# Attention before a mixture of experts: five instruction queues in one fixed table per pair of heads, clusters chosen for two heads at once

## The chip, the cores and the metric

The program runs on one core of one Trainium2 chip. The metric is the device time of one execution in microseconds (us), lower is better. Five engines work side by side, each through its own queue in order: PE (TensorE, the matmuls), DVE (VectorE), ACT (ScalarE), POOL (GpSimd) and SP (SyncE, which here only issues DMAs). In the profile PEld are PE's weight loads and SPq and POOLq are the DMA-issuing parts of SP and POOL.

## The reference

Three stages follow each other. The first is attention in which a query sees only the keys of its own cluster; its output feeds a dense layer (512 to 2048 and back) and a mixture of 8 experts.

```python
B, H, S, D, n_clusters = 2, 8, 768, 64, 16
q_assign = argmax(q_n @ c_n.T, axis=-1)         # nearest of 16 centroids, per head
k_assign = argmax(k_n @ c_n.T, axis=-1)
mask = q_assign[:, :, :, None] == k_assign[:, :, None, :]
scores = where(mask, q @ k.T / sqrt(D), -1e9)
attn = exp(scores - max(scores)); attn /= attn.sum(-1) + 1e-9
x = attn @ v                                     # then x -> [B*S, H*D] = [1536, 512]
x = silu(x @ moe_w_in) @ moe_w_out
out = sum over 8 experts of P[:, e] * (relu(x @ w1[e]) @ w2[e])   # P: Sinkhorn-normalised gate
```

## The kernel before

There are 16 heads (2 batches of 8). A head has 768 queries and 768 keys, and its scores are worked on in six tiles of 128 queries by 768 keys; the whole attention stage is 96 such tiles. Two heads make a pair, and the output of a pair fills 128 rows of the transposed activations `xh`, `xl` (a rounded number and its remainder, as everywhere in this kernel where float32 accuracy is reached with two fp32r operands).

The steps of a head, with the names that the profile shows and their lines:

- `load` (L137, L139) brings keys and queries to `raw` (128 x 768: 64 rows of keys, 64 of queries) and the values to `vr`. `cast` scales the queries on POOL (L155), rounds by a DMA from POOL's queue (L156) to slot 2 of `qk`, and copies the other slots by three DMAs on SP (L158, L159). `split` takes the remainder on POOL (L169) and places it with two DMAs on SP (L170, L171).
- `assign` (L219): similarity `sim` of each of six groups of 128 positions with the head's centroids: the 128 x 128 block of `raw` is the stationary operand, 32 columns of `chl` (the centroids of keys and of queries) move. `choose` (L232 to L237) takes the maximum over 16, marks it, picks one mark and writes `oh`, a one-hot row per position.
- `mask_transp` (L243) turns `oh` with six PE transposes into `oht`, of which 48 rows are used, and `mask_rows` copies 16 rows of it into slot 3 and, scaled by 2**60 and shifted by -2**60, 16 rows into slot 2 of `qk` (ACT, L248 and L252; DVE L250 for head 0). These 16 extra contraction rows put the mask into the scores.
- `scores` (L269, L270): four matmuls of 384 columns for a tile, two for each half of the keys: one with 128 contraction rows, one with 80, of which the last 16 are the mask. The tile `s` lies in one of two PSUM buffers. `rowmax` (DVE L275) and `expo` (ACT L284) follow, and the exponentials free the PSUM buffer. When both tiles of a chunk are through, `normalise` works out `rec` (DVE L289, L290) and scales `p` on POOL (L293).
- `transp` (PE L303): three units of four 128 x 128 transposes per chunk, through three PSUM buffers `t`; `evac` copies them to `pt` (two units on ACT, one on DVE).
- `av` (L334): for each third of the queries 12 matmuls (24 instructions in the profile) with 64 stationary columns, the two heads of a pair alternating; then `xh` on ACT (L346) and `xl` on DVE (L347).

What sets the order: the main loop at the end of the stage walks over the tiles and calls the steps at fixed distances before the head that needs them (`AHEAD`), and the scheduler of the framework then places the instructions on each engine by its own estimate of when they are ready, in this stage and the next. `SEQ` runs the tiles of heads 0 and 1 one after the other and from then on alternates between the two heads of a pair by thirds. The first weight block of the dense layer is fetched and split in this stage as well (`wload`, `narrow`, `wsplit`): two of its four pieces in the first 35 us.

After the stage the pools are closed and the dense layer begins (L456, `l`), then the experts (L706).

## Time and profile before

| | |
|---|---|
| runs of the program | 1538.35, 1540.16, 1540.43 us; median 1540.16 us |
| the profiled execution | 1541.73 us |
| its span, from the first to the last instruction | 1539.9 us |
| mean granted TensorE clock | 0.998 |
| attention, up to the first matmul of the dense layer | 288.27 us |
| dense layer and experts | 1251.6 us |
| busy share of the span | PE 97%, PEld 86%, DVE 70%, ACT 59%, POOL 32% |

The profile gives the instructions of one execution with start and duration, and for each idle stretch of an engine what ended it. A PE duration includes the passage through the array, so durations of matmuls that follow each other overlap; the distance from start to start is what one of them costs in a row of many. The granted clock is the share that the throttle grants; whether the array runs at its lower level (1.2 GHz) or its higher (2.4 GHz) shows in that distance.

### The profile page before, as it was taken

The numbers are of one execution on the slowest core, as the hardware profiler recorded it, in microseconds if no ns is written. First come the engines' busy times: TensorE is split into PE (matmuls) and PEld (weight loads), VectorE is DVE, ScalarE is ACT, GpSimd is POOL, SyncE is SP. The second block draws the span as 40 slices with busy tenths as digits, with TensorE's granted clock in tenths as the row PEclk, the third lists the DMA queues.
The fourth block names the chain that finished last, engine by engine and source line by source line (L and its number), as shares of the span: only waits on it lengthen the run. The fifth ranks groups of instructions, "written<-read, shape, count | busy, mean of one in ns | idle before, by whom it ended". The sixth has DMA issues, their size and how long they took to land.

```text
span 1539.9 us, 24994 instructions
## 1 busy us (share of the span) xinstructions
PE 1495.0 (97%) x9768; PEld 1328.9 (86%) x9768; DVE 1080.1 (70%) x1680; ACT 910.0 (59%) x1732; POOL 485.8 (32%) x429
## 2 busy tenths in 40 slices
PE   5999999999999999999899999999999999999997
PEld 4777777777888878999899999999999999999997
DVE  5765666689778268877586685775776866866857
ACT  3766767432342337575665765865766756757654
POOL 5765554465665400125411211201201202112111
PEclk9999999999999999999999999999999999999999
DMA  6444442122110102668877958759759559569575
GB/s 205 138 131 122 123 109 98 29 69 96 55 55 1 55 1 74 154 114 224 151 132 141 147 94 157 128 96 174 114 95 188 96 104 193 86 120 166 87 138 103
DMA packets 131334, 175.66 MB, mean 114 GB/s; under 512 B 5456, under 2 KB 100944, under 8 KB 131216
## 3 DMA queue, kind: packets, MB, share of 16 engines
q0 software_dynamic: 82976, 86.91, 36.9%
q1 hardware_dynamic: 48096, 87.13, 17.9%
q8 instruction: 77, 1.26, 0.3%
q14 instruction: 41, 0.34, 0.1%
q10 hardware_dynamic: 144, 0.03, 0.0%
HBM read 64.54 MB, written 88.87 MB: 100 GB/s over the span
## 4 chain that ended last, share of the span: by engine, by line
PE 82%; DVE 8%; POOL 4%; DMA 2%; issue 2%; ACT 1%; POOLq 0%; DVEq 0%; SPq 0%; ACTq 0%
PE b L706 29%; PE a L706 29%; PE l L456 13%; PE av L334 3%; PE t L303 3%; PE s L269 2%; PE s L270 1%; DVE m L275 1%; DMA out_dram<-acc 1%; PE sim L219 1%; POOL p L293 1%; POOL raw L169 1%; ACT p L284 1%; PE gl L649 0%; DVE acc L794 0%
## 5 line engine op out<-in xcount | busy, mean ns | idle before, releaser
L819 POOL DMA_DIRECT2D out_dram<-acc x101 | 146.6, 1724 | 755.8 <-ACT acc L813 503.8
L706 PE MATMUL b<-wfh,ah 128*128 128x256 f32 x1344 | 381.9, 284 | 2.2 <-ACT acc L813 1.8
L706 PE MATMUL b<-wfl,ah 128*128 128x256 f32 x1344 | 381.3, 284 | 0.2 <-DVE wfl L529 0.2
L706 PE MATMUL b<-wfh,al 128*128 128x256 f32 x1344 | 381.1, 284 | 0.0
L706 PE MATMUL a<-xfh,wfh 128*128 128x512 f32 (+1 forms) x896 | 303.6, 339 | 4.2 <-ACT acc L813 1.8
L706 PE MATMUL a<-xfl,wfh 128*128 128x512 f32 (+1 forms) x896 | 303.1, 338 | 0.0
L706 PE MATMUL a<-xfh,wfl 128*128 128x512 f32 (+1 forms) x896 | 301.8, 337 | 0.9 <-DVE wfl L529 0.9
L706 PEld LDWEIGHTS b<-wfh,ah 128*128 128x128 f32 x1344 | 258.3, 192 | 3.6 <-ACT acc L813 2.3
L706 PEld LDWEIGHTS b<-wfl,ah 128*128 128x128 f32 x1344 | 258.3, 192 | 0.9 <-DVE wfl L529 0.4
L706 PEld LDWEIGHTS b<-wfh,al 128*128 128x128 f32 x1344 | 258.3, 192 | 0.0
L813 ACT ACTIVATE acc<-b,Pg 128x256 f32<-128x256 f32 x484 | 188.3, 494 | 30.7 <-issue 18.8
L756 ACT CAST ah<-h 128x768 fp32r<-128x768 f32 x192 | 159.0, 862 | 66.4 <-DVE h L838 26.3
L706 PEld LDWEIGHTS a<-xfh,wfh 128*128 128x128 f32 x896 | 170.3, 190 | 24.3 <-ACT acc L813 2.5
L529 DVE TENSOR_TENSOR al<-h,ah 128x768 fp32r<-128x768 f32 x192 | 177.2, 957 | 19.4 <-ACT ah L756 18.8
L706 PEld LDWEIGHTS a<-xfh,wfl 128*128 128x128 f32 x896 | 169.9, 190 | 19.9 <-DVE wfl L529 1.4
L706 PEld LDWEIGHTS a<-xfl,wfh 128*128 128x128 f32 x896 | 170.4, 190 | 16.7
L529 DVE TENSOR_TENSOR wfl<-w0r,wfh 128x512 fp32r<-128x512 f32 x96 | 64.8, 689 | 82.4 <-ACT wfh L604 80.3
L526 DVE TENSOR_TENSOR h<-a,h 128x512 f32<-128x512 f32 x144 | 94.2, 685 | 26.7 <-PE a L706 25.6
L275 DVE TENSOR_REDUCE m<-s 128x1 f32<-128x768 f32 x96 | 91.4, 953 | 29.6 <-PE s L270 28.7
L284 ACT ACTIVATE p<-s,m 128x768 f32<-128x768 f32 x96 | 86.9, 906 | 40.1 <-DVE rec L290 16.5
L293 POOL TENSOR_SCALAR p<-p,rec 128x768 f32<-128x768 f32 x96 | 86.8, 915 | 71.4 <-DVE rec L290 43.7
L743 ACT COPY h<-a 128x512 f32<-128x512 f32 x144 | 80.7, 591 | 45.6 <-PE a L706 45.5
(189 smaller groups left out, 2693.4 us busy)
## 6 DMA issues: line engine op xcount, KB each, us to landing
out_dram<-acc POOLq DMA_DIRECT2D x101, 768.0 KB, 9.9
w0r<-in_w_dram SPq DMA_DIRECT2D x16, 1024.0 KB, 8.1
w1r<-in_w_dram SPq DMA_DIRECT2D x16, 1024.0 KB, 6.8
qk<-qk SPq DMA_DIRECT2D x45, 192.0 KB, 3.3
raw<-in_w_out_dram SPq DMA_DIRECT2D x8, 1024.0 KB, 4.9
raw<-in_kq_dram SPq DMA_DIRECT2D x16, 384.0 KB, 3.8
raw<-in_w_in_dram SPq DMA_DIRECT2D x6, 1024.0 KB, 5.2
out_dram<-acc SPq DMA_DIRECT2D x8, 768.0 KB, 4.0
```

The source lines that it names most:

```text
L275: nc.vector.tensor_reduce(out=m, in_=tiles[i]["s"][:, :, :CH], axis=AX.XY, op=ALU.max, negate=True)
L284: nc.scalar.activation(p, t.pop("s")[:, :, :CH], AF.Exp, bias=t.pop("m"), accum_out=chunks[c]["sum"][:, j : j + 1])
L293: nc.gpsimd.tensor_scalar(out=p, in0=p, scalar1=ck["rec"][:, j : j + 1], scalar2=1.0, op0=ALU.mult, op1=ALU.mult)
L303: nc.tensor.transpose(ps[:, b * P : (b + 1) * P], p[:, kt * P : (kt + 1) * P], ident)
L456: nc.tensor.matmul(ps, lhsT=s(k), rhs=m(k), start=n == 0, stop=n == 11)
L526: e.tensor_tensor(out=out, in0=in0, in1=in1, op=op)
L529: e.tensor_tensor(out=lo, in0=x, in1=r(hi), op=ALU.subtract)
L706: nc.tensor.matmul(ps[bank][:, cols], lhsT=lf(i, k), rhs=rt(j, k), start=first and bank not in opened, stop=k == 1 and q == 2, skip_group_ ...
L743: act.copy(bank(t, u), ps[u])
L756: act.copy(hi, x)
L813: act.mul(t[:, 2 * u + m], z[:, m], g)
L819: gps.dma_start(out=out_block(i, j), in_=t, accum_op=ALU.add)
```

## The change

Only the attention stage is touched. The order of the instructions of dense layer and experts is the same, row for row, on every engine.

1. The stage is written by hand for all five queues, SP's included, and no longer placed by the scheduler. A text table `ORDER` names 135 steps; it is the same for each pair of heads. An entry `T,-6` in pair k is step number 18k - 6 of its kind, so that entries with negative numbers finish the pair before, and `sim,1`, `castm,4` and the like prepare the next pairs. `where_is` alternates the heads of a pair from the first pair on.
2. The similarity of both heads is taken together (`simil`): now the centroids are stationary, 32 columns, and `raw` moves, 384 columns at a time; the four results go to four strips of 32 partitions of one PSUM bank. A copy to SBUF (`sims`) and three transposes (`simt`) bring it to positions by rows, and `cha` to `che` choose for both heads in operations of twice the width.
3. `oh` holds both heads in 128 columns: six transposes (`oht`) per pair in place of twelve. One ACT operation (`mr`) scales all 128 rows into `mk` in SBUF, and four DMAs of 16 rows (`md`, on SP) place them in the `qk` slots. The mask row is now -2**60 times "not in this cluster" instead of a scaled and shifted one-hot row.
4. `scores` cuts the 768 keys into 512 and 256 columns instead of twice 384.
5. Of the 18 transposed units of a pair 11 are copied by ACT and 7 by DVE (before 12 and 6). Buffers: `raw` 4 (before 3), `vr` 6 (5), `pt` 4 (6).
6. The prologue issues 12 matmuls on a constant tile (`warm`), and 12 more at four places before the first scores, and 4 after each of tiles 1 and 3 (`FILL`). `make_identity`, the cast of it and the constants stand in another order, and the two early weight pieces leave the prologue: all four pieces are fetched and split, one per pair, in pairs 1 to 6.

```diff
-    SEQ = [(g, t) for g in range(2) for t in range(NCH)] + [(g + o, t) for g in range(2, NH, 2) for t in range(NCH) for o in range(2)]
+    def where_is(c):
+        k, o = divmod(c, 2)
+        pair, third = divmod(k, NTHIRD)
+        return 2 * pair + o, third
...
-        for i in range(NT):
-            nc.tensor.matmul(
-                hd["sim"][:, i].rearrange("p a c -> p (a c)"),
-                lhsT=hd["raw"][:, i * P : (i + 1) * P],
-                rhs=chl[:, hd["h"]].rearrange("p a c -> p (a c)"),
...
+    def simil(q, where=False):
+        ps = half_bank(q, "sim", where and q > 1)
+        for j in range(2):
+            for o in range(2):
+                row = 32 * (2 * j + o)
+                cl = chl[:, (2 * q + o) % H].rearrange("p a c -> p (a c)")
+                nc.tensor.matmul(ps[row : row + 32, :CH], lhsT=cl, rhs=raw[2 * q + o][:, j * CH : (j + 1) * CH], start=True, stop=True, skip_group_check=True)
+        sim[q] = ps
+
+    def sims(q):
+        t = ap.tile([P, CH], F32, name=f"sims{q}", tag="sims", bufs=1)
+        nc.scalar.copy(t, sim[q][:, :CH])
+        sim[q] = t
+
+    def simt(q, where=False):
+        ps = half_bank(q, "simt", where)
+        for b in range(CH // P):
+            nc.tensor.transpose(ps[:, b * P : (b + 1) * P], sim[q][:, b * P : (b + 1) * P], ident)
...
+    def oht(q, where=False):
+        po = half_bank(q, "oht", where).bitcast(BF16)
         for i in range(NT):
+            nc.tensor.transpose(po[:, i * P : (i + 1) * P], onehot[q % 2][:, 2 * (i % 3) + i // 3, :], identb)
+        rows[q] = po
+
+    def mr(q):
+        mk = ap.tile([P, S], F32R, name=f"mk{q}", tag="mk", bufs=1)
+        nc.scalar.activation(mk, rows.pop(q)[:, :S], AF.Copy, scale=msc)
+        rows[q] = mk
+
+    def md(q):
+        mk = rows.pop(q)
+        for o in range(2):
+            for a, slot in enumerate((3, 2)):
+                row = 64 * o + 32 * a
+                nc.sync.dma_start(out=r(qk[2 * q + o][D : D + C, slot, :]), in_=r(mk[row : row + C]))
...
-        for c in range(2):
-            nc.tensor.matmul(ps[:, c, :CH], lhsT=t[:, 1, qt * P : (qt + 1) * P], rhs=t[:, 0, c * CH : (c + 1) * CH], start=True, stop=False)
-            nc.tensor.matmul(ps[:, c, :CH], lhsT=t[: D + C, 3, qt * P : (qt + 1) * P], rhs=t[: D + C, 2, c * CH : (c + 1) * CH], start=False, stop=True)
+        for ks in (slice(0, 512), slice(512, S)):
+            nc.tensor.matmul(ps[:, ks], lhsT=t[:, 1, qt * P : (qt + 1) * P], rhs=t[:, 0, ks], start=True, stop=False)
+            nc.tensor.matmul(ps[:, ks], lhsT=t[: D + C, 3, qt * P : (qt + 1) * P], rhs=t[: D + C, 2, ks], start=False, stop=True)
...
+    ORDER = """
+        S,0 xh,-2 xl,-2 nrm,-2 T,-6 mx,0 T,-5 nrm,-1 S,1 evA,-5 evD,-6 ex,0 T,-4 mx,1 castm,4 sim,1,1 T,-3 evA,-4 wp1,-3 ex,1 T,-2 evD,-3 T,-1 sims,1
...
+    with tc.manual_schedule(engines={ENG.PE, ENG.DVE, ENG.Activation, ENG.Pool, ENG.SP}):
...
+        def warm(n):
+            for _ in range(n):
+                nc.tensor.matmul(wps, lhsT=wm[:, :P], rhs=wm, start=True, stop=True)
+
+        FILL = {1: 4, 3: 4}
+        PTB = 4
+        warm(12)
+        make_identity(nc, ident)
...
+        for pair in range(-4, NPAIR + 4):
+            for item in ORDER:
+                kind, at, *place = item.split(",")
+                f, stride, low, high = KINDS[kind]
+                i = int(at) + stride * pair
+                if low <= i < high:
+                    f(i, *(bool(int(w)) for w in place))
```

How the rows move. First PE at the very start of the program; in these rows `s` are scores, `pc` the transposed centroids, `sim` similarities, `oht` the transposed one-hot rows, `wm` and `wps` the constant tile and its target. Before, from the first instruction:

```order
L269 MATMUL s_194<-qk_109 128x384
L269 MATMUL s_235<-qk_109 128x384
L200 MATMUL pc<-ident,cn_134 128x128
L219 MATMUL sim_161<-chl,raw_93 128x32 x6
L243 LDWEIGHTS oh_143
L243 MATMUL oht_175<-identb,oh_143 48x128
```

Now, from the last of the first 12 constant matmuls on:

```order
L398 LDWEIGHTS wm
L398 MATMUL wps<-wm 128x512
L446 MATMUL pc<-ident,cn_175 128x128
L398 LDWEIGHTS wm
L398 MATMUL wps<-wm 128x512
L189 MATMUL sim_183<-raw_90,chl 32x384
L189 MATMUL sim_183<-raw_92,chl 32x384
L189 MATMUL sim_183<-raw_90,chl 32x384
L189 MATMUL sim_183<-raw_92,chl 32x384
```

Before, the first halves of two score tiles stood ahead of everything and the similarities of head 0 came alone, those of heads 1 and 2 after its `oht`. Now no scores stand there, and four matmuls serve heads 0 and 1 together.

Second, PE in the middle of the stage, where the similarities of a later head or pair are taken; `t` are the transposed exponentials. Before:

```order
L303 MATMUL t_1378<-ident,p_1288 128x128 x4
L269 MATMUL s_1393<-qk_843 128x384
L270 MATMUL s_1393<-qk_843 128x384
L269 MATMUL s_1393<-qk_843 128x384
L270 MATMUL s_1393<-qk_843 128x384
L219 MATMUL sim_1408<-chl,raw_1274 128x32 x6
L243 LDWEIGHTS oh_143
L243 MATMUL oht_1415<-identb,oh_143 48x128
```

Now:

```order
L264 MATMUL s_571<-qk_232 128x512
L265 MATMUL s_571<-qk_232 128x512
L264 MATMUL s_571<-qk_232 128x256
L265 MATMUL s_571<-qk_232 128x256
L300 MATMUL t_583<-ident,p_500 128x128 x4
L189 MATMUL sim_591<-raw_238,chl 32x384
L189 MATMUL sim_591<-raw_352,chl 32x384
L189 MATMUL sim_591<-raw_238,chl 32x384
L189 MATMUL sim_591<-raw_352,chl 32x384
L300 MATMUL t_596<-ident,p_540 128x128 x4
```

Before, the similarities of one head stood directly ahead of the mask transposes of another, after a score tile; this came twice in a pair. Now they come once in a pair, between two units of transposes, and the mask transposes stand elsewhere.

Third, SP's queue in the middle of the stage. Before, with L158 and L159 the copies of the rounded operand, L170 and L171 the remainders and L137 and L139 loads:

```order
L158 DMA qk_843<-qk_843 64x768 x2
L159 DMA qk_843<-qk_843 64x768
L170 DMA qk_843<-raw_702 64x768
L171 DMA qk_843<-raw_702 64x768
L158 DMA qk_1025<-qk_1025 64x768 x2
L159 DMA qk_1025<-qk_1025 64x768
L137 DMA raw_1274<-in_kq_dram 128x768
L170 DMA qk_1025<-raw_897 64x768
L171 DMA qk_1025<-raw_897 64x768
```

Now, with L172 and L173 the copies, L180 and L181 the remainders, L251 the mask rows:

```order
L160 DMA vr_1412<-in_vp_dram 128x384
L172 DMA qk_1361<-qk_1361 64x768 x2
L173 DMA qk_1361<-qk_1361 64x768
L156 DMA raw_1456<-in_kq_dram 128x768
L180 DMA qk_1209<-raw_905 64x768
L181 DMA qk_1209<-raw_905 64x768
L251 DMA qk_1209<-mk_1554 16x768 x2
L251 DMA qk_1361<-mk_1554 16x768 x2
L180 DMA qk_1361<-raw_1080 64x768
L181 DMA qk_1361<-raw_1080 64x768
```

The mask rows of both heads of the next pair are new on this queue, behind the remainder of the one head and ahead of that of the other; copies and remainders of a head are no longer neighbours.

## Rows read from the trace of the kernel before

**Rows 1.** The page: the chain that ended last, by engine.

```profile
PE 82%; DVE 8%; POOL 4%; DMA 2%; issue 2%; ACT 1%; POOLq 0%; DVEq 0%; SPq 0%; ACTq 0%
```

**Rows 2.** Timeline of PE: start, duration, line, operation; single score matmuls, tail, dense layer.

```profile
23.04 0.67 PE L270 MATMUL s<-qk 80*128 80x384 f32 x1
...
56.08 0.42 PE L270 MATMUL s<-qk 80*128 80x384 f32 x1
...
251.22 0.34 PE L270 MATMUL s<-qk 80*128 80x384 f32 x1
...
276.86 0.34 PE L270 MATMUL s<-qk 80*128 80x384 f32 x1
...
288.27 0.50 PE L456 MATMUL l<-xh,wh 128*128 128x512 f32 x1
```

**Rows 3.** Stretches: us, busy of PE, PEld, DVE, ACT, POOL; clock, DMA.

```profile
24.40:56.10 31.70, 25.98 (x139) 22.70 (x138) 21.19 (x41) 19.71 (x38) 21.51 (x22) 1.00 0.61 168
56.10:277.20 221.10, 216.58 (x1560) 168.79 (x1558) 139.16 (x286) 151.34 (x300) 125.96 (x136) 1.00 0.40 114
```

**Rows 4.** Timeline of PE, 159 to 168 us.

```profile
159.85 2.80 PE L334 MATMUL av<-pt,vr 128*64 128x256 f32 x22
162.59 0.44 PE L269 MATMUL s<-qk 128*128 128x384 f32 x1
...
163.40 1.48 PE L303 MATMUL t<-ident,p 128*128 128x128 f32 x12
164.63 0.42 PE L269 MATMUL s<-qk 128*128 128x384 f32 x1
...
165.43 1.42 PE L219 MATMUL sim<-chl,raw 128*128 128x32 f32 x12
166.78 0.52 PE L243 MATMUL oht<-identb,oh 128*48 128x128 bf16 x6
```

**Rows 5.** Timeline of PE in the experts, rows of 512 and 256 columns.

```profile
699.77 0.39 PE L706 MATMUL a<-xfh,wfh 128*128 128x512 f32 x1
...
701.13 0.28 PE L706 MATMUL a<-xfh,wfh 128*128 128x256 f32 x1
...
702.56 0.40 PE L706 MATMUL a<-xfh,wfh 128*128 128x512 f32 x1
```

**Rows 6.** Timeline of POOL, DVE, PE and ACT at the start.

```profile
4.80 0.57 POOL L184 TENSOR_TENSOR cst<-cst,pw 128x1 f32<-128x1 f32 x1 [2.71 <-DVE cst L183]
...
7.48 0.14 DVE L186 TENSOR_SCALAR cst<-cst 128x1 f32<-128x1 f32 x1
...
9.41 0.45 PE L200 MATMUL pc<-ident,cn 128*128 128x128 f32 x1 [0.96 <-DVE cn L198]
...
10.48 2.77 PE L219 MATMUL sim<-chl,raw 128*128 128x32 f32 x12 [0.62 <-DMA raw<-in_w_in_dram]
...
13.29 0.36 DVE L232 TENSOR_REDUCE sm<-sim 128x12 f32<-128x192 f32 x1 [1.85 <-PE sim L219]
...
17.13 0.83 PE L243 MATMUL oht<-identb,oh 128*48 128x128 bf16 x6 [3.88 <-DVE oh L237]
...
18.00 0.79 ACT L248 CAST qk<-oht 16x768 fp32r<-16x768 bf16 x1 [2.51 <-PE oht L243]
```

**Rows 7.** The page: the costliest groups; count, busy, mean ns, idle before.

```profile
L275 DVE TENSOR_REDUCE m<-s 128x1 f32<-128x768 f32 x96 | 91.4, 953 | 29.6 <-PE s L270 28.7
L284 ACT ACTIVATE p<-s,m 128x768 f32<-128x768 f32 x96 | 86.9, 906 | 40.1 <-DVE rec L290 16.5
```

**Rows 8.** Timeline of PE where the clock shows: 41 to 45 us and 346 us.

```profile
41.81 0.52 PE L269 MATMUL s<-qk 128*128 128x384 f32 x1
...
44.78 0.34 PE L269 MATMUL s<-qk 128*128 128x384 f32 x1
...
346.66 0.47 PE L456 MATMUL l<-gh,wh 128*128 128x512 f32 x1 [2.72 <-DVE acc L489]
```

**Rows 9.** Waits of SP's queue, 42 to 290 us: total, times, longest.

```profile
SPq L170 <- POOL raw L169: 61.7, 12, 9.2
```

More of the change, by code (lines that the diff above doesn't have):

```diff
@@ L111, in wsplit, with wsplit_steps @@
+    def wsplit_steps(n, k, pool):
         tag = "ab"[n % 2]
@@ L287, in normalise, with rec @@
-    def normalise(c):
+        t["p"] = ap.tile([P, S], F32, name=f"p{i}", tag="p", bufs=7)
+        nc.scalar.activation(t["p"], t.pop("s")[:, :S], AF.Exp, bias=t.pop("m"), accum_out=chunks[c]["sum"][:, j : j + 1])
+    def rec(c):
         ck = chunks[c]
@@ L381, in units @@
[L381 to L414 removed]
+        avs[k] = ps
@@ new lines, in x_of, with xhi, xlo, wd @@
+    def x_of(k):
+        pair, third = divmod(k, NTHIRD)
+        b, kc = divmod(pair, KC)
+        return kc, slice(b * S + third * CW, b * S + (third + 1) * CW)
+    def xhi(k):
+        kc, ts = x_of(k)
+        nc.scalar.copy(xh[:, kc, ts], avs[k][:, :CW])
+    def xlo(k):
+        kc, ts = x_of(k)
+        nc.vector.tensor_tensor(out=xl[:, kc, ts], in0=avs.pop(k)[:, :CW], in1=r(xh[:, kc, ts]), op=ALU.subtract)
+    def wd(k):
+        wload(0, k, 1, pp, 2)
+    def wstep(key):
+        def one(k):
+            if k not in steps:
+                steps[k] = wsplit_steps(0, k, pp)
+            f = steps[k].get(key)
+            if f:
+                f()
+        return one
```

417 lines of the change are left out of this document (200 added, 217 removed).

## The prediction

> **What bounds the kernel now.** I read the chain of waits first: 82% of what ended last is PE [rows 1], so time is won only where PE has less to do or waits less. Second, the order of instructions: dense layer and experts keep theirs, so only the stretch up to the dense layer's first matmul at 288.27 us can move. Third, the timeline of PE cuts it. A pair has 24 of the L270 matmuls, and counting them gives: pair 0 begins at 23.04, pair 1 at 56.08, pair 7 at 251.22, the last one stands at 276.86, the dense layer begins at 288.27 [rows 2]. So 23.0 us of start, 33.0 for pair 0, 195.1 for pairs 1 to 6 (32.5 each), 25.6 for pair 7 and 11.4 of tail.
>
> Fourth: how full is PE in those 32.5 us? The stretch view says 216.6 of 221.1 us busy [rows 3], but these durations overlap (the twelve transposes there last 1.48 us and the next matmul starts 1.23 us after them), so I add distances from start to start [rows 4]. A score tile: 162.59 to 163.40, 0.81 us, 12 of them 9.7. Twelve transposes: 163.40 to 164.63, 1.23, six times 7.4. One third of `av`: 22 records in 2.74, 24 in 2.99, three times 9.0. Similarities: 1.35 per head, 2.7. Mask transposes: at most 0.52 per head, 1.0. Sum 29.8 us of 32.5: 2.7 us per pair PE stands still in small gaps, with the array at its higher clock. The other engines are not full there: DVE 63%, ACT 68%, POOL 57% [rows 3].
>
> **The start.** The first scores need the centroids, the similarities, the choice and the mask rows. The power on POOL ends at 5.37, but DVE takes up its result only at 7.48, after two long operations on `qk` and a cast; the new order puts these elsewhere, 2.1 us less. From 7.48 to the transpose of the centroids 1.93 and on to the similarities 1.07 stay [rows 6], so these start at 8.4. Similarities for two heads: 1.5 us (below). New behind them are the copy to SBUF (0.5 to 0.8, ACT is free by then) and three transposes (0.35 at 0.1 each): 10.9. The choice took 13.29 to 17.13, 3.84 us, with pieces of the weight split between its steps; these go, the operations become twice as wide: 3.6, with 3.0 and 4.8 as ends. Mask transposes to copy 0.87, copy 0.8 to 0.95 [rows 6]: first L265 matmul (the old L270) at 16.8 instead of 23.04, bounds 15.5 and 20. The 12 + 12 constant matmuls run where PE waits anyway. If a batch is late, at worst the six ahead of `oht` stand in its way, 6 x 0.23 = 1.4 us by the pace of 512 columns [rows 5].
>
> The early weight pieces, which leave the prologue, cost nothing later: one piece per pair adds to DVE, ACT and POOL in four pairs, and these had 10 to 14 us of 32.5 free [rows 3].
>
> **The clock in the start.** At 41.81 a score matmul lasts 0.52, at 44.78 the same 0.34 [rows 8]: before, the array was at 1.2 GHz until 44.5 us, after a start with many holes, and at 2.4 GHz from then on. The constant matmuls fill the holes, and I take it that pair 0 runs at 2.4 GHz. The Trainium skill, "TensorE: Matmul & The Clock Gate" ("Why this matters for your kernels"), warns that an idle gap sends the clock back to the lower level. Here, a gap of 2.72 us left the next matmul in the row at 0.47, not the 0.52 of the narrower one at the low level [rows 8]; the largest hole left in the new start is the choice, 3.6 us less up to 1.4 of filling, about the same. That it falls back is a rival below.
>
> **A pair.** Part by part, against the 29.8 us:
> - Score tiles: 512 columns cost (701.13 - 699.77) / 6 = 0.227, 256 cost (702.56 - 701.13) / 12 = 0.119 [rows 5], two of each 0.69. Four of 384 cost 0.71 at the pace within a tile (0.81 less the step into it, about 0.1). 0.02 less, 12 times: 0.2.
> - Similarities: no row shows 32 stationary and 384 moving columns. Nearest is `av`, also float32 in two records and with two column halves of the array alternating: 0.1245 per record of 256 columns [rows 4], 0.187 for 384, 8 records 1.5 us. If the four strips do not overlap, twice that, 3.0; if all four do, 0.75. I take 1.5, from the nearest row. With the three transposes 1.8 instead of 2.7: 0.9 less, bounds -0.6 and +1.6.
> - Mask transposes: 6 instead of 12, 0.5 less.
> - Transposes and `av` stay. Sum 28.2.
>
> "TensorEngine Tiling (Array Packing)" of the Trainium skill, Key Properties, speaks against the new similarities: a change of tiling mode drains TensorE, and they stand between two units of transposes, two changes more per pair. In the trace the tile after `av`, which also uses part of the columns, costs 0.81 and the one after transposes 0.80 (164.63 to 165.43) [rows 4]; a drain of this kind shows as 0.01 us, so the sum is the same by rule and row.
>
> The gaps: the old ones come from a scheduler's estimates. I walked the table once through a pair with the durations of the rows (0.81 tile, 0.95 maximum, 0.91 exponential [rows 7]). Two tiles in flight need 2.9 us for PSUM to turn over, and between each two score tiles the table puts other PE work of about that length; the third of `av` stands behind each pair of adjacent tiles, and its last operands come 0 to 1 us ahead of it. So the walk finds no lasting stall but margins near zero, and I take 1.1 us of gaps, less than half of the old 2.7 (ends 0 and 2.7): 29.3 us per pair.
>
> Loads of the others per pair stay below that. The long stretch holds 221.1 / 32.5 = 6.8 pairs, so ACT had 151.3 / 6.8 = 22.3 us; it loses a unit copy and four row copies of 0.8, gains one row operation and one copy: 20. DVE 20.5, gains one unit copy, 21. POOL 18.5 stays. A weight piece adds a few us to each [rows 3].
>
> SP's queue gets four small DMAs per pair. They stand behind the remainder of a head, which waits for POOL; before, these waits were 5.1 us each on average, 9.2 at most [rows 9]. In the walk the mask rows land about 2 us before the scores of the next pair want them; nothing is late while POOL keeps its place.
>
> **The sum.** Start 23.0 to 16.8. Pair 0: 33.0 to 25.0, that is 29.3 less six transpose units (2.5) and a third of `av` (3.0) that have no predecessor, plus 1.2 for the first maximum, exponential and scaling that nothing covers (bounds 24 and 30). Pairs 1 to 6: 195.1 to 175.8. Pair 7: 25.6 to 24.0, since similarities, mask and the last `av` fall away. Tail: one third of `av`, six units, the last copy, one third of `av` and handovers, 11.4 to 9.9. Together 251.5 instead of 288.3: 36.8 us less. The dense layer needs its second weights from the start; their loads stand behind the last pair's preparation, a whole pair ahead, so they are there and it begins as before.
>
> The profiled execution was 1541.73 us, 1.57 above the median of the runs. 1541.7 - 36.8 = 1504.9; less 1.6 gives 1503.3, rounded 1504.
>
> **Rivals.**
> 1. The gaps stay as they were: the table only moves them, since a pair waits for the same handovers. For it: nearly empty margins in my walk. Against: the old order was made for heads that were prepared one by one. A pair takes 28.2 + 2.7 = 30.9; over 6.7 pairs (pairs 1 to 7, the last shorter) 11 us of the gain are gone: 1515.
> 2. The table packs without a gap and the four strips overlap fully: 27.5 to 28.0 per pair, 9 to 12 us more gain: 1494. For it: the walk; against: the semaphores between engines are in no row of mine.
> 3. The clock falls back in the choice and pair 0 starts at 1.2 GHz, as before. Then its transposes and `av` cost about double until it rises; the old pair 0 at that level took 8 us more than I give the new one, and it would add up to these 8: 1512. It is what the rule above of the Trainium skill on the clock would give.
> 4. Slower: the mask rows come late. Place: `md` on SP behind `sd`, which waits for `split` on POOL, behind two scalings of a chunk; everything after `md` on SP waits with it, the next pair's scores for the rows, and then all engines. It decides from 2 us of lateness; each us beyond costs one us in each of 7 handovers. To eat 36.8 us it must be 5.3 + 2 = 7.3 us late each time: 1540, and more with the longest wait of the old queue, 9.2 us, 1554. For it: waits of that size stand on this queue today. Against: then they were hidden and a step was prepared less far ahead; a full POOL is not to be seen.
>
> **Chances.** Forecast (29.3 give or take 0.8 per pair) 0.50, its own range 1497 to 1512; rival 1, with worse gaps up to the old period, 0.23; rival 2 0.12; rival 3 0.07; rival 4 0.08. About 0.2%, 3 us, is what a measurement of this kernel can tell from no change. Slower 0.06 and same 0.03 come from rival 4 and from the worst of rival 1 with a late start; faster 0.91. The range takes in rivals 1 and 3 and nearly all of 2: low, 28.0 per pair and a start of 15.5, 1504 - 6.7 x 1.3 - 1.3 = 1494, with a little for overlapping strips 1492; high, the old 32.5 per pair with the start and tail as forecast, 1504 + 6.7 x 3.2 = 1525, with a little for a slow pair 0, 1528.
>
> **What would show it.** In the timeline of PE: first L265 at 16.8; one sixth of the distance from pair 1's first to pair 7's first at 29.3 (30.9 speaks for rival 1, 28 for rival 2); four similarity matmuls within 1.5 us; score matmuls of 256 columns 0.28 long and not some 0.4 in pair 0 (else rival 3); first dense matmul at 251.5 and 1251.6 us behind it unchanged. In the waits of SP's queue `md` behind POOL's `split`, and the first score of a pair released by a DMA, would be rival 4. I am wrong at the root if pairs still take over 32 us, or if the dense layer waits for its weights.

## The result, and the profile after

| | before | changed |
|---|---|---|
| time, median (range) | 1539.26 (1536.29 to 1540.43) us | 1500.89 (1497.13 to 1504.18) us |
| ratio to before, 95% interval | | 0.9753 [0.9722, 0.9783] |
| profiled execution, its span | 1541.73, 1539.9 us | 1504.18, 1502.4 us |
| attention, up to the dense layer | 288.27 us | 250.17 us |
| dense layer and experts | 1251.6 us | 1252.2 us |

Faster by 38 us, all of it in the attention stage, 3 us from the forecast of 1504. The chain of waits of the changed kernel, beside [rows 1]:

```profile
PE 83%; DVE 10%; DMA 2%; POOL 1%; issue 1%; ACT 1%; DVEq 0%; POOLq 0%; ACTq 0%
```

The timeline of PE at the places of [rows 2]: first score matmul of pair 0, pair 1 and pair 7, last score matmul, dense layer.

```profile
16.66 0.79 PE L265 MATMUL s<-qk 80*128 80x512 f32 x1 [0.99 <-DVE qk L471]
...
44.46 0.40 PE L265 MATMUL s<-qk 80*128 80x512 f32 x1
...
217.92 0.39 PE L265 MATMUL s<-qk 80*128 80x512 f32 x1
...
240.48 0.28 PE L265 MATMUL s<-qk 80*128 80x256 f32 x1
...
250.17 0.50 PE L523 MATMUL l<-xh,wh 128*128 128x512 f32 x1
```

So 16.7 us of start, 27.8 for pair 0, 173.5 for pairs 1 to 6, 22.6 for pair 7 up to the last score matmul and 9.7 of tail. In the kernel before, [rows 2] has the second L270 of pairs 1 and 7 in place of the first; counted again, these pairs begin a little earlier:

```profile
54.93 0.34 PE L270 MATMUL s<-qk 80*128 80x384 f32 x1
...
250.86 0.34 PE L270 MATMUL s<-qk 80*128 80x384 f32 x1
```

So there pair 0 took 31.9 us and not 33.0, and a pair 32.7 and not 32.5. The forecast does not hang on it, as its new parts were built up anew. By these starts the change took 6.4 us off the start, 4.1 off pair 0, 22.5 off pairs 1 to 6, 3.4 off pair 7 and 1.7 off the tail.

The six pairs are not alike. Counting the L265 matmuls gives 27.43, 28.03, 30.37, 29.82, 30.37, 27.44 us: pairs 2 to 5 carry DVE's steps on the weight pieces, and three of them are 2.4 to 2.9 us longer than pairs 1 and 6. What PE waits for between 44 and 241 us (total, times, longest):

```profile
PE oht L238 <- DVE oh L233: 4.7, 6, 1.0
PE s L264 <- ACT p L281: 3.1, 2, 1.6
PE simt L200 <- DVE xl L343: 2.1, 3, 1.5
```

The first comes in each of pairs 1 to 6, the others only in the long ones. SP's queue, beside [rows 9], still waits for POOL's `split`, but no wait of PE hangs on it:

```profile
SPq L180 <- POOL raw L176: 50.7, 6, 10.0
```

A piece of the middle, beside [rows 4]: tile 0.82 us from 99.58, the eight records of the similarities 0.78 from 102.52, and 24 records of `av` 2.82 from 96.76.

```profile
96.76 2.89 PE L322 MATMUL av<-pt,vr 128*64 128x256 f32 x24
99.58 0.50 PE L264 MATMUL s<-qk 128*128 128x512 f32 x1
...
100.40 1.04 PE L300 MATMUL t<-ident,p 128*128 128x128 f32 x8
...
102.52 0.85 PE L189 MATMUL sim<-raw,chl 128*32 128x384 f32 x8
103.30 0.88 PE L300 MATMUL t<-ident,p 128*128 128x128 f32 x6
```

The start, beside [rows 6, 8]. PE stands still for 2.38 us in the choice and again ahead of the first L265; behind that 512 columns cost 0.43 us from start to start, nearly twice the 0.24 of 22.82: the array is at 1.2 GHz from there up to about 22.3 us.

```profile
14.28 0.51 PE L238 MATMUL oht<-identb,oh 128*128 128x128 bf16 x6 [2.38 <-DVE oh L233]
...
17.67 0.63 PE L264 MATMUL s<-qk 128*128 128x512 f32 x1
18.10 0.63 PE L265 MATMUL s<-qk 80*128 80x512 f32 x1
...
22.82 0.40 PE L265 MATMUL s<-qk 80*128 80x512 f32 x1
23.06 0.28 PE L264 MATMUL s<-qk 128*128 128x256 f32 x1
```

DVE in pair 2 and pair 3, the same operation:

```profile
78.42 0.50 DVE L106 TENSOR_SCALAR n_0u<-raw 128x512 uint32<-128x512 uint32 x1
...
107.43 2.90 DVE L106 TENSOR_SCALAR n_1u<-raw 128x512 uint32<-128x512 uint32 x1
```

And POOL beside it. In pair 2 the operation got in between two scalings of POOL, and these last 1.95 us together instead of 1.78. In pair 3 it did not, and the subtraction of the piece before follows the scalings at once. Why it got in the one time and not the other, these rows don't show.

```profile
77.74 1.95 POOL L291 TENSOR_SCALAR p<-p,rec 128x768 f32<-128x768 f32 x2 [0.45 <-DVE rec L286]
...
107.01 1.78 POOL L291 TENSOR_SCALAR p<-p,rec 128x768 f32<-128x768 f32 x2
108.76 1.27 POOL L129 TENSOR_TENSOR wl<-n_0b,wh 128x512 fp32r<-128x512 f32 x1
```

L106 ends at 110.33, 0.3 us behind POOL's run: a wait inside an instruction, which no view of waits lists.

### The profile page after: what moved, and what is told of

Same layout as the page of the kernel before. It is cut to its first block, busy times and chain, and to the rows that moved or that the text cites. A ratio compares the mean times of both kernels' runs of the same rounds, so it can differ in the third digit from the quotient of the medians.

```text
span 1502.4 us, 24709 instructions
## 1 busy us (share of the span) xinstructions
PE 1464.2 (97%) x9647; PEld 1302.2 (87%) x9648; DVE 1104.6 (74%) x1665; ACT 891.0 (59%) x1710; POOL 485.3 (32%) x425
## 3 DMA queue, kind: packets, MB, share of 16 engines
q1 hardware_dynamic: 48992, 88.50, 18.7%
## 4 chain that ended last, share of the span: by engine, by line
PE 83%; DVE 10%; DMA 2%; POOL 1%; issue 1%; ACT 1%; DVEq 0%; POOLq 0%; ACTq 0%
PE b L773 30%; PE a L773 30%; PE l L523 13%; PE t L300 3%; PE av L322 2%; DVE m L272 2%; PE s L264 1%; PE s L265 1%; DMA out_dram<-acc 1%; DVE oh L233 1%; PE gl L716 0%; DVE h L593 0%; DVE acc L861 0%; DMA raw<-in_w_in_dram 0%; DVE al L596 0%
## 5 line engine op out<-in xcount | busy, mean ns | idle before, releaser
L880 ACT ACTIVATE acc<-b,Pg 128x256 f32<-128x256 f32 x484 | 188.6, 495 | 30.3 <-issue 18.7
L596 DVE TENSOR_TENSOR wfl<-ws,wfh 128x512 fp32r<-128x512 f32 x48 | 33.5, 697 | 88.1 <-ACT wfh L671 88.1
```

The source lines that it names most:

```text
L596: e.tensor_tensor(out=lo, in0=x, in1=r(hi), op=ALU.subtract)
L880: act.mul(t[:, 2 * u + m], z[:, m], g)
```

## The experiments

Each is the changed kernel with one edit, unless said otherwise. Dense layer and experts, the same in all of them, took 1246.8 to 1252.4 us in the thirteen profiled executions of changed kernels; that scatter is in every time, so the verdicts on a part go by the stage's own starts (us, from the timeline of PE). The stage scatters as well: the changed kernel, e2, e3 and e7 have the same table and differ in the start alone, and in them pairs 1, 2 and 6 agree within 0.1 us, but pairs 3 to 5 differ by up to 1.3. In the edits below, the names of the table are: `S` a score tile, `mx` its maximum, `ex` its exponential, `nrm` the scaling on POOL, `T` four transposes, `evA` and `evD` their copy by ACT or DVE, `ld` a load of keys and queries, `castm` the scaling of the queries on POOL, `split` the remainder on POOL, `sd` its DMAs, `cha` to `che` the choice, `w0` to `w4` DVE's steps on a weight piece and `wp2` POOL's subtraction for it; the number behind the comma counts as in the change's first point.

| run | first L265 | pair 0 | pairs 1 to 6 | dense from | time | ratio to before, 95% |
|---|---|---|---|---|---|---|
| changed | 16.66 | 27.80 | 27.43 28.03 30.37 29.82 30.37 27.44 | 250.17 | 1500.89 | 0.9753 [0.9722, 0.9783] |
| e1 | 17.56 | 28.07 | 27.48 28.03 29.05 28.82 30.56 27.44 | 249.26 | 1499.56 | 0.9749 [0.9729, 0.9768] |
| e2 | 18.66 | 26.14 | 27.43 28.05 29.09 30.27 30.17 27.44 | 249.50 | 1503.33 | 0.9769 [0.9747, 0.9790] |
| e3 | 17.71 | 31.13 | 27.48 28.02 29.27 30.28 29.79 27.46 | 253.39 | 1503.85 | 0.9767 [0.9743, 0.9791] |
| e4 | 18.56 | 29.00 | 27.41 28.00 31.72 28.88 30.06 27.41 | 253.27 | 1499.51 | 0.9738 [0.9719, 0.9757] |
| e5 | 16.81 | 28.71 | 26.93 27.28 28.81 29.07 29.47 26.96 | 246.28 | 1501.57 | 0.9751 [0.9732, 0.9771] |
| e6 | 17.04 | 29.10 | 27.49 27.45 29.04 28.53 28.05 27.44 | 246.39 | 1495.49 | 0.9718 [0.9699, 0.9737] |
| e7 | 16.02 | 24.51 | 27.43 28.07 29.49 30.34 29.35 27.47 | 244.92 | 1496.87 | 0.9728 [0.9706, 0.9750] |
| e8 | 16.89 | 24.46 | 26.93 27.05 28.40 27.97 28.39 26.97 | 239.30 | 1491.07 | 0.9691 [0.9674, 0.9708] |
| e9 | 16.48 | 26.29 | 26.95 27.28 28.45 28.28 28.75 26.96 | 241.68 | 1495.60 | 0.9710 [0.9688, 0.9732] |
| e10 | 25.08 | 31.01 | 31.19 27.88 26.95 26.93 26.93 26.94 | 255.15 | 1505.17 | 0.9785 [0.9761, 0.9808] |
| e11 | 17.02 | 30.21 | 27.45 28.66 31.08 31.85 29.00 27.43 | 254.95 | 1506.64 | 0.9784 [0.9765, 0.9803] |
| e12 | 17.67 | 30.65 | 29.81 30.40 30.41 30.41 30.40 29.82 | 261.83 | 1513.85 | 0.9833 [0.9809, 0.9857] |

**e1: two operands instead of one**, in `w0`, and likewise in `w1` with a constant tile, for the first weight block.

```diff
-w0=lambda: ts(out=ui("u"), in0=high, scalar1=0x7FFFFFFF, scalar2=None, op0=ALU.bitwise_and),
+w0=lambda: v.scalar_tensor_tensor(out=ui("u"), in0=high, scalar=0x7FFFFFFF, in1=high, op0=ALU.bitwise_and, op1=ALU.bitwise_and),
```

> The changed kernel (1500.9 us) with one edit: the first two of DVE's steps on a weight piece (w0, L106, and w1, L107) are written with two SBUF operands, at the same places of the table. Pairs 1 to 6 of the changed kernel last 27.43, 28.03, 30.37, 29.82, 30.37 and 27.44 us; pairs 2 to 5 carry the same weight steps. In pair 2 L106 lasts 0.50 us, in pairs 3 and 5 2.90 and 2.89, in pair 4 L107 lasts 2.82, and in these three POOL runs two scalings and a subtraction without a pause over the same 3 us. Theory A (collision): an operation of DVE with one operand that comes up while POOL goes from one instruction to the next without a pause does not begin until POOL pauses; one with two is not held (L110, 0.91 us beside POOL's L291 and L176). Then L106 and L107 last about 0.9 us each, pairs 3 to 5 come to 28.0 to 28.4 us and the time to 1494 to 1497. Theory B (volume): the pairs are long because DVE has more work in them; then they get 0.5 to 0.9 us longer still: 1502 to 1505. Theory C: operations with two SBUF operands are held as well; nothing is gained, L106 or L107 lasts about 3 us: 1501 to 1504. The Trainium skill, SBUF - State Buffer (the doors of the SBUF), would give theory C, since it counts operations with two SBUF inputs among those that wait for a GpSimd operation that reads SBUF.

Measured: pairs 3 and 4 come to 29.05 and 28.82, pair 5 stays at 30.56. There DVE shows the operation (L110 in this kernel) at 3.17 us, beside POOL's unbroken run:

```profile
166.40 3.17 DVE L110 SCALAR_TENSOR_TENSOR n_3u<-raw 128x512 uint32<-128x512 uint32 x1
```

```profile
165.98 1.79 POOL L295 TENSOR_SCALAR p<-p,rec 128x768 f32<-128x768 f32 x2
167.74 1.27 POOL L133 TENSOR_TENSOR wl<-n_2b,wh 128x512 fp32r<-128x512 f32 x1
```

Theory A's half on two operands is refuted, theory C's mechanism is right: such an operation is held as well. By that rule of the Trainium skill nothing should be gained. In pairs 3 and 4 the operation came up at other moments of POOL's run and took 0.69 and 0.75 us; the shorter pair 3 is within the scatter (29.09 in e2), pair 4 is 1.0 us under the least of the kernels with the same table.

**e6: the weight steps at another place.**

```diff
-rec,0 S,3 wh,-3 mx,2 nrm,0 av,-1 w0,-2 nrm,1 ex,2 mx,3 wp2,-3 w1,-2 ex,3 w2,-2 S,4
+rec,0 S,3 wh,-3 mx,2 nrm,0 av,-1 nrm,1 ex,2 mx,3 w0,-2 w1,-2 ex,3 w2,-2 w3,-2 S,4
-ex,7 w3,-2 split,2
+ex,7 split,2
-castm,5 evD,9
+castm,5 wp2,-3 evD,9
```

> The changed kernel with the weight steps at other places of the table: w0, w1, w2 and w3 of DVE together behind mx,3, where POOL pauses 1.7 us in a pair without weight work, and POOL's wp2 behind castm,5, where it pauses 1.7 us as well, no longer behind nrm,1. Theory A (collision): the 2.8 to 3.2 us that L106, L107 or (written with two operands) L110 last in pairs 3 to 5 come from POOL's run of three instructions, scaling, scaling, wp2; with the run cut, they last 0.4 to 0.9, pairs 3 to 5 come to 27.9 to 28.5 and the stage is 5 to 7 us shorter, 1494 to 1497. Theory B (volume): the same work in the same pairs makes the same 30 us, 1500 to 1502.

Measured: the first step lasts 0.53, 2.15, 2.07 and 0.80 us in pairs 2 to 5, none 2.8 or more, and these pairs 27.45, 29.04, 28.53, 28.05 instead of 28.03, 30.37, 29.82, 30.37: 5.5 us less with the same work in the same pairs, and still 4.2 less than the shortest of e2, e3 and e7. Volume (theory B) is out as the cause of these. The edit moves DVE's steps and POOL's `wp2` at once, so it does not tell which of the two moves gave how much. What is left stands where POOL's two scalings still run beside the step, pair 3:

```profile
108.92 2.15 DVE L106 TENSOR_SCALAR n_1u<-raw 128x512 uint32<-128x512 uint32 x1
```

**e5: `split,2` away from the choice.**

```diff
-w3,-2 split,2 S,8 che,1
+w3,-2 S,8 che,1
-ex,4 split,3 mx,5
+ex,4 split,3 split,2 mx,5
```

> The changed kernel with one step of the table at another place: split,2 (POOL, the remainder of the next pair's first head) stands directly behind split,3 and no longer ahead of che,1. In the changed kernel the two operations of che (L233, two SBUF operands) take 2.24 us in the middle of the stage, where POOL's L176 begins 0.5 us ahead of them, and 0.63 in the start, where POOL is between two instructions; and PE waits 4.7 us for them in six pairs (oht <- DVE oh). Theory A (collision): an operation of DVE with two SBUF operands stands still while POOL works on SBUF; with split,2 gone from that place che takes 0.7 to 1.5 us (the scalings of nrm,5 may still stand beside it), oht comes 0.8 to 1.5 us earlier, and each of pairs 1 to 6 gets 0.6 to 0.9 us shorter: 26.5 to 26.9 for pairs 1 and 6, 1495 to 1498 in all. Theory B (che is slow because its operands are slow to read): the 2.24 us stay, and nothing changes, 1500 to 1502. Theory C: split,2 earlier pushes chc and the scalings behind it back by 0.8 us and these become the late ones: 1500 to 1506, PE waiting for POOL's p.

Measured: L233 takes 0.53 us on average instead of 1.17 between 44 and 241 us, pairs 1 and 6 last 26.93 and 26.96, all six are 4.9 us shorter together, of which 1.7 lie in pairs 1, 2 and 6, which hardly scatter. Theory A, with 0.5 us in a pair a little under the 0.6 to 0.9 expected. Over the stage the two operations show it (in the changed kernel 345/423/1977, in the last section):

```profile
L233 DVE TENSOR_TENSOR oh<-ss,sm x16: 344/348/974, 13.8 to 204.6; 128x192 bf16<-128x192 f32 x16
```

The time, 1501.6, missed the 1495 to 1498 expected and does not show the gain: its scatter is larger.

**e2 and e3: the constant matmuls.** e2 issues none of them; e3 issues more around the choice:

```diff
-        simt(0)
-        warm(6)
+        simt(0)
+        warm(14)
...
-            f(0)
-        warm(3)
+            f(0)
+        warm(7)
```

> The changed kernel without any of the matmuls on the constant tile: neither the 24 of the prologue nor the 8 after tiles 1 and 3. Theory A (the constants keep the array at its higher level in the start): without them the eight similarity records cost 1.44 us instead of 0.89, the three transposes some 0.4 more and the transpose of the centroids 0.2 more, the first L265 comes at 17.5 to 18 instead of 16.66, and pair 0 runs at the lower level far beyond 22.3 us, where the changed kernel rises; before the change that level lasted to 44.5 us and I allowed 8 us for it. Time 1504 to 1510. Theory B (they do little): the changed kernel falls to the lower level at 16.7 us in spite of them, and the eight after tiles 1 and 3 cost 0.47 us each there, 3.8 us; without them the level rises at about the same time by the work itself, and the time is 1497 to 1500.

> The changed kernel with more matmuls on the constant tile around the choice of the first pair: 14 instead of 6 ahead of the mask transposes and 7 instead of 3 behind them. In the changed kernel PE stands still for 2.38 us ahead of oht (14.28) and 0.99 ahead of the first L265 (16.66), and behind them 512 columns cost 0.43 us instead of 0.23, up to 22.3 us. Theory A (the two holes bring the lower level): with the holes filled at 0.235 us per matmul (14 end at 13.7, 7 more at 16.3) the first two tiles, the four constants and the similarities behind them cost 2.5 to 3 us less; first L265 at 16.6 to 17.0, pair 0 25 us, time 1497.5 to 1499. Theory B: the level falls all the same, and the added matmuls, at 0.4 each, push oht and the scores back by 2 to 4 us: 1503 to 1505.

Measured in e2: the start is 2.0 us later, more than the 0.8 to 1.3 of theory A, partly because L233 is held in the choice (0.98 us instead of 0.36). But the array rises at 25 us by the work itself and pair 0 is 1.7 us shorter; pair 1 begins at 44.80 against 44.46. As they stand, the constants bring nothing that can be told in the stage: theory B. The time, 1503.3, lies between the two theories. In e3 the array stays at 2.4 GHz as theory A wanted (256 columns at 0.12 us from 18.04 to 24.5), and pair 0 is 3.3 us longer all the same:

```profile
18.04 0.28 PE L264 MATMUL s<-qk 128*128 128x256 f32 x1
...
28.75 1.97 PE L300 MATMUL t<-ident,p 128*128 128x128 f32 x8 [3.96 <-POOL p L291]
30.36 0.78 PE L264 MATMUL s<-qk 128*128 128x512 f32 x1
```

Neither theory had that. POOL stands ahead of the scalings in the preparation of head 4, whose load was issued late:

```profile
26.36 0.83 POOL L163 TENSOR_SCALAR raw<-raw 64x768 f32<-64x768 f32 x1 [9.48 <-DMA raw<-in_kq_dram]
```

PE waits 3.96 us, and the array is at the lower level again (512 columns at 0.58 and 0.42 us from 30.36 on).

**e7: another start.**

```diff
-        warm(6)
-        split(1)
-        sd(1)
+        warm(13)
...
-        warm(3)
+        nc.vector.tensor_tensor(out=raw[1].bitcast(F32R), in0=raw[1], in1=r(qk[1][:, 2, :]), op=ALU.subtract)
+        ld(4)
+        sd(1)
+        warm(7)
```

> The changed kernel with another start: the remainder of head 1 (split(1), POOL) goes to DVE behind che(0); the load of head 4 is issued ahead of sd(1) and not behind the copies of head 2; 13 constant matmuls instead of 6 ahead of oht and 7 instead of 3 behind it. In the run with the filled choice the array stayed at the higher level (256 columns at 0.12 us from 18.04 to 24.5), but pair 0 lasted 31.1 us, since L233 took 2.17 us beside POOL's L176, and PE then waited 4.0 us for POOL's p, because POOL stood behind castm of head 4, whose load landed at 26.3 us; PE's next matmul was at the lower level again. Theory A: three things set the start, the collision in the choice, the late load and the level; with all three gone the first L265 comes at 16.0 to 16.3 (16.66 to 18.6 in the runs so far), POOL scales from 22 us on, and pair 0 lasts 23.5 to 25 us instead of 26 to 31: pair 1 begins at 40 to 41, 3 to 4 us ahead of the changed kernel, 1496.5 to 1498. Theory B: the array falls back at another hole, and the start goes as in the changed kernel: pair 1 begins at 44 to 45, 1500 to 1502.

Theory A in all three points. First L265 16.02, PE's hole in the choice 0.28 us, no low level, pair 0 24.51, pair 1 at 40.53:

```profile
13.65 0.51 PE L238 MATMUL oht<-identb,oh 128*128 128x128 bf16 x6 [0.28 <-DVE oh L233]
...
16.36 0.28 PE L264 MATMUL s<-qk 128*128 128x256 f32 x1
...
19.39 0.40 PE L265 MATMUL s<-qk 80*128 80x512 f32 x1
```

From the first L265 to that of tile 2 this start takes 3.37 us, the changed kernel 6.16 (16.66 to 22.82): 2.8 us are what the lower level costs in these tiles.

**e8: e5, e6 and e7 together.**

> The changed kernel with the three edits together: split,2 behind split,3, the weight steps behind mx,3 and castm,5, and the new start. If each gives what its theory A says: first L265 at 16 to 16.3, pair 0 24 to 25 us, pairs 1, 2 and 6 26.5 to 26.9, pairs 3 to 5 27.2 to 28, tail as it was: dense layer from 236 to 239 us instead of 250.2, time 1487 to 1490. If one of the edits takes back what another gives (the scalings on POOL later by 0.8 us, mask rows or remainders late on SP), 1492 to 1500.

Measured: 1491.07 us (1490.94 to 1493.63), the stage 10.9 us shorter than in the changed kernel; 1.1 above the upper end for all gains in full, since the weight pairs 3 to 5 stay at 28.0 to 28.4 and the first L265 comes at 16.89, later than in e7. PE no longer waits for the choice; L106 still takes 2.14 us beside the scalings. It beats both kernels.

**e9: the first weight steps once more elsewhere.** On top of e8:

```diff
-T,-1 sims,1 evD,-2
+T,-1 sims,1 w0,-2 w1,-2 w2,-2 evD,-2
-mx,3 w0,-2 w1,-2 ex,3 w2,-2 w3,-2 S,4
+mx,3 ex,3 w3,-2 S,4
-simt,1,1 ld,5
+simt,1,1 ld,5 wd,-1
-rec,5 wd,-1
+rec,5
```

> The run with all three edits (1491.1 us; dense layer from 239.30; pairs 26.93, 27.05, 28.40, 27.97, 28.39, 26.97), with w0, w1 and w2 once more at another place: after the second maximum and the copies of a pair, where POOL pauses 2.4 us, and no longer behind mx,3, where L106 still lasts 2.14 us beside POOL's two scalings; w3 stays behind mx,3; the load of the next weight piece is issued in the middle of the pair instead of at its end, since the operation comes 4 us earlier. Theory A: what is left of the weight steps' price (3 x 1.3 us) is that one operation standing still; with it gone pairs 3 to 5 come to 27.1 to 27.5, the dense layer begins at 235.5 to 237, 1487 to 1489. Theory B: the steps now hold up the copies and rec,0 behind them by 1.3 us, and the pairs stay at 28 or get longer: 1491 to 1493.

Theory B: the pairs stay at 28.3 to 28.8, and PE waits for ACT's exponentials instead (3.4 us, six times). The place is no better. That it is worse is not shown: pairs 2 to 5 are 1.0 us longer together, no more than they scatter, and 1.8 of the 2.4 us by which the dense layer begins later lie in pair 0, which the edit leaves alone and where PE waits 1.80 us for a DMA to `qk`.

**e10: the scheduler in place of the table.**

```diff
-    with tc.manual_schedule(engines={ENG.PE, ENG.DVE, ENG.Activation, ENG.Pool, ENG.SP}):
+    with ExitStack():
```

> The changed kernel with the same steps, written in the same sequence, but without the fixed order: the scheduler places the instructions of the stage on all five engines, as before the change. It tells what of the 21.6 us in pairs 1 to 6 and of the start comes from the table and what from the smaller work. Theory A (the table closes the gaps): the old gaps of 2.7 us per pair come back, pairs last 30 to 31, and the constant matmuls are pulled ahead of the real ones; dense layer from 268 to 275 us, 1518 to 1526. Theory B (the work is what counts): PE's work per pair is 26.6 us whoever orders it, pairs stay under 28.5, 1498 to 1505. Theory C: the steps with their small buffers (three of t, one of mk and sims) fit the scheduler badly: over 1530.

Theory B in the pairs, with the time at its upper end: from pair 3 on, where no weight work is left, the scheduler's pairs last 26.93 to 26.95, as short as the table's shortest (26.93 in e5 and e8), and PE has no idle time in them (stretch; PE busy first, then the other engines):

```profile
142.11:222.91 80.80, 80.80 (x629) 66.00 (x627) 62.59 (x117) 57.57 (x121) 50.05 (x53) 1.00 0.49 131
```

It loses the start. The weight steps are drawn into the choice and pairs 0 to 2, and there 6.35 us of PE are gone:

```profile
20.45 0.82 PE L238 MATMUL oht<-identb,oh 128*128 128x128 bf16 x6 [6.35 <-DVE oh L233]
```

**e4: 384 and 384 columns**, the cut of before.

```diff
-for ks in (slice(0, 512), slice(512, S)):
+for ks, d in ((slice(0, CH), slice(0, CH)), (slice(512, 512 + CH), slice(CH, S))):
```

> The changed kernel with the score tiles cut into 384 and 384 columns (two PSUM banks, 384 columns of each) instead of 512 and 256, as before the change; the maximum and the exponential read the two parts. Theory A (my term): four matmuls of 384 cost 0.71 us against 0.69, 0.02 per tile or 0.2 us per pair: 1.5 us over the stage, 1502 to 1503. Theory B: the cut is worth more, because a pair is bound by PE and the step from one matmul to the next counts too: 0.1 per tile, 9 us, 1510. Theory C: nothing, 1500 to 1501.

Theory C: the pairs that nothing else disturbs last 27.41, 28.00 and 27.41 against 27.43, 28.03 and 27.44.

**e11: the mask rows later on SP.**

```diff
-nrm,7 evD,7 md,1 ex,8
+nrm,7 evD,7 ex,8
-T,11 sd,3 mx,10
+T,11 sd,3 md,1 mx,10
```

> The changed kernel with the four DMAs of the mask rows (md) behind the remainder of the second head (sd,3) on SP, 1.2 us later, to size the margin of my rival 4. In the changed kernel they are issued from 93.04 to 96.30 in one pair and land 3.0 us behind the issue, 99.3, and the first L265 of the next pair stands at 99.92. Theory A (the margin is what these rows show, 0.6 us): the last rows land at 100.5, each of the seven handovers has a wait of PE for a DMA of 0.5 to 0.8 us, 3.5 to 5.5 us in all, 1504.5 to 1506.5. Theory B (the margin is the 2 us that I took in the prediction): no wait, 1500 to 1502.

Between the theories: one of the seven handovers is late, by 0.38 us (0.72 instead of 0.34 from L264 to L265), the others not; pairs 1 and 6 keep their length.

```profile
102.62 0.50 PE L264 MATMUL s<-qk 128*128 128x512 f32 x1
103.34 0.47 PE L265 MATMUL s<-qk 80*128 80x512 f32 x1 [0.22 <-issue]
```

The margin is larger than the expectation had it. The first tile of a pair needs the rows of the first two of the four DMAs. In the changed kernel the second is issued at 93.64 and lands 3.6 us later, at 97.3, 2.7 us ahead of the L265 at 99.92; over the seven handovers this margin is 1.6 to 4.2 us. In e11 the four land a median 4.2 us behind their issue instead of 3.0, and the margin shrinks to 0.1 to 3.4; in the late pair the second DMA, issued at 97.44, lands 5.8 us later, just ahead of the L265 at 103.34. So the 2 us of the prediction were about right. The rest of the 4.8 us by which the dense layer begins later lies in pair 0 and the weight pairs, which vary in every run.

**e12: mask rows by ACT**, in place of `mr` and `md`.

```diff
-nc.scalar.activation(mk, rows.pop(q)[:, :S], AF.Copy, scale=msc)
+for o in range(2):
+    for a, slot in enumerate((3, 2)):
+        row = 64 * o + 32 * a
+        nc.scalar.activation(qk[2 * q + o][D : D + C, slot, :], po[row : row + C, :S], AF.Copy, scale=(1.0, -BIG)[a])
```

> The changed kernel with the mask rows placed by four ACT copies of 16 rows out of PSUM instead of one scaling of 128 rows on ACT and four DMAs on SP. Theory A (ACT has room, but not there): the copies take 4 x 0.8 = 3.2 us instead of 0.9, and the exponential and the copies of t behind them come 2.3 us later, at a place where PE waits for nothing else; half of it or all reaches PE: 1.2 to 2.3 us in each of six pairs, 1508 to 1515. Theory B (hidden): ACT is busy 20 of 27.4 us and catches up within the tile; 1500 to 1503. Theory C: better than before, since the rows are in place at once and not 3 us after an issue: below 1499.

Theory A, at its upper end: 2.4 us more in each of pairs 1, 2 and 6. PE stands still for 1.14 us in the middle of twelve transposes and goes on with them at 101.77, just behind the four copies, which end at 101.62. From the first of the twelve to the next score tile it is 3.2 us (99.97 to 103.18), in the changed kernel 1.2 (93.50 to 94.73):

```profile
98.34 3.28 ACT L246 ACTIVATE qk<-oht 16x768 fp32r<-16x768 bf16 x4 [1.99 <-PE oht L238]
```

```profile
101.77 1.18 PE L298 MATMUL t<-ident,p 128*128 128x128 f32 x8 [1.14 <-POOL raw L163]
```

The profile names an operation of POOL that ended at the same time and has nothing to do with these transposes; what they share with the copies is the PSUM buffer of `oht`, one of three. That it is the buffer is read from the code and not tested.

## Why the prediction was right, and where its steps were not

**The start** (16.8, measured 16.66) was right, but with luck. Its terms add up to 16.2 or 16.3 (10.9 + 3.6 + 0.87 and 0.8 to 0.95), not to 16.8, and the twelve executions other than e10 give 16.0 to 18.7, partly by where POOL's remainder of head 1 falls on the choice.

**"I take it that pair 0 runs at 2.4 GHz"** failed, as rival 3 had it: up to about 22.3 us the array is at the lower level. That costs 2.8 us (beside e7) and not 8, since PE goes on with only one hole, of 0.24 us, and the level is back by then. But pair 0 is not long by the clock alone, and this the prediction did not have. The first transposes need POOL's scalings; what these need from DVE (`rec`) is ready at 21.6 us, but POOL stands ahead of them in the preparation of head 4, whose load lands at 23.9:

```profile
24.04 0.83 POOL L163 TENSOR_SCALAR raw<-raw 64x768 f32<-64x768 f32 x1 [8.57 <-DMA raw<-in_kq_dram]
...
25.48 3.56 POOL L291 TENSOR_SCALAR p<-p,rec 128x768 f32<-128x768 f32 x4
```

e11 has the start of the changed kernel, and in it the level did not fall ahead of the scores (256 columns 0.28 us long at 17.36). PE then waited for these scalings instead, the level fell behind that wait, and pair 0 took 30.2 us:

```profile
26.93 1.97 PE L300 MATMUL t<-ident,p 128*128 128x128 f32 x8 [2.82 <-POOL p L291]
```

e3, with the holes filled, shows the same. Pair 1 begins at 44.5 in the changed kernel, at 47.2 and 48.8 in e11 and e3 with the level kept up to the wait, and at 40.5 in e7 with the level kept and the load early. So the 25.0 for pair 0 lacked two terms, the level and POOL's place in its queue, and filling the holes is worth nothing without the early load. What the early load is worth by itself was not run.

**A pair: 28.2 of work and 1.1 of gaps, 29.3.** The average is 28.9, but neither addend was right: the work is 26.9 (e10, where PE never stands still from pair 3 on; the shortest pairs of e5 and e8 are as long), the rest 2.0. The similarities cost 0.78, not 1.5, which is the 0.75 of four strips that overlap fully, rival 2's half. `av` was 2.99 per third, scaled from 22 records to 24; it is 2.74 to 2.82. The 22 were eleven matmuls: the twelfth stood apart in the old order, and eleven took 2.74 us, as long as twelve take now. That neighbours overlap because they write to different halves of the columns would give this; no run tests it. The kernel before, in another pair:

```profile
136.08 0.65 PE L334 MATMUL av<-pt,vr 128*64 128x256 f32 x2
136.65 0.66 PE L303 MATMUL t<-ident,p 128*128 128x128 f32 x4
...
138.38 2.81 PE L334 MATMUL av<-pt,vr 128*64 128x256 f32 x22
141.12 0.44 PE L269 MATMUL s<-qk 128*128 128x384 f32 x1
```

**"The gaps: the old ones come from a scheduler's estimates"** was wrong. Before the change PE waited for another engine 4.4 us in 6.8 pairs (the row below and 0.3 more), 0.65 per pair and not 2.7. The other 2 us were work in pieces, like the 0.57 us above. Between 120.59 and 153.09 us, one pair, distances from start to start give 9.9 us for `av` against the 9.0 of my sum, 8.8 for the transposes against 7.4, 0.6 of it a wait, and 10.1 for the score tiles against 9.7; similarities and mask transposes are within 0.1 of the sum.

```profile
PE s L269 <- ACT p L284: 4.1, 6, 1.2
```

Given the new steps, the same scheduler leaves no gap from pair 3 on (e10). What the fixed table adds is the start and the first pairs. In pairs without weight work it is the worse order, 27.43 against 26.94, by the place of one step: with `split,2` moved, the table comes to 26.93 as well (e5).

**"The early weight pieces ... cost nothing later"** was the edit costed at nothing that had a price: 8.9 us in pairs 2 to 5 (118.6 together, against four times the 27.43 of pair 1). The cover, free time on DVE, was there; the instruction stood still in it. e6 takes 4.2 to 5.5 us of the price away by place alone. Rival 1's period, nearly reached in three of the pairs, came by this and not by handovers.

**Mask rows** (rival 4) did not come late; against my margin of 2 us the landings show 1.6 to 4.2 (e11). That moving them off ACT matters I had counted as room, 20 of 29 us; undone it costs 2.4 us per pair (e12). **512 and 256 columns** were given 1.5 us and bring none (e4).

So the total was right because errors of both signs met: a pair's work was 1.3 too high and its gaps 0.9 too low, pair 7 was 1.4 too high (24.0, measured 22.6), and pair 0 2.8 too low. That leaves 1.3 us in the stage. The rest of the 3 us is that the profiled execution lies 3.3 us above the median and not the 1.6 that I took off. Left open: the scheduler's order from pair 1 on behind e7's start, by the rows 16.0 + 24.5 + 6 x 26.9 + 22.6 + 9.7 = 234 us, without a price for the weight steps, which e10 paid before pair 3; it was not tried.

## What to carry to other kernels

Cost a moved operation by what runs beside it on the neighbour engine, not by the free time of its own: look for one instruction whose duration differs from its twins, since such a wait stands in no list of waits. And before a gap is put down to an order, read what PE waited for there: a unit of work cut in pieces looks like idle time in a sum made from whole ones.
